# Starting every large SBUF tile at a multiple of 128 bytes in a fused attention and two-layer feed-forward kernel

## The chip, the cores and the metric

One core of one Trainium2 chip. The metric is device time in microseconds (us), the median of three runs. The engines are TensorE (PE, its weight loads listed as PEld), VectorE (DVE), ScalarE (ACT), GpSimd (POOL) and SyncE (SP), which issues nearly all DMAs.

## What is computed

Local attention with a few global keys over 4 batches, 8 heads, 768 positions and 64 head columns, and then two feed-forward layers on the 3072 x 512 result:

```python
scores = q @ k.T / 8 + bias          # bias: -slope[h] * distance
keep   = is_global | is_local        # 8 global keys, a window of 96
a      = softmax(where(keep, scores, -1e9))
x      = (a @ v) as [3072, 512]
h = x @ w1_in;  y   = (h - tanh(h)) @ w1_out     # w1_in [512, 2048]
h = y @ w2_in;  out = (h * cos(h)) @ w2_out      # w2_out [2048, 512]
```

## The kernel before

All arithmetic is float32. The feed-forward products split each operand into a high part in the type float32r and a low part (value minus high), and add three products: high x high, high x low, low x high. So each chunk of weights is a tile `w` of [128, 2, 512] (tags `wi` and `wo`, 16 buffers each), and each chunk of activations is a pair as well (`xt`, `x`, `g`).

The work goes in four phases. Phase 0 is the attention, with the first half of layer one (f chunks 0 to 7) woven into it in 12 blocks of 256 tokens: `h<-xt,wi` (L561) and `c<-g,wo` (L615), 12 matmuls of 256 columns per chunk each. A list scheduler (`Plan`, L49) with written costs and due times sets the order on each engine, and `in_order` (L32) pins it. Phases 1 to 3 are the other half of layer one and the two halves of layer two, in 6 blocks of 512 tokens and 8 chunks each: `h<-x,wi` (L561), then `o<-g,wo` (L615, phase 1) or `o<-wo,g` (L619, phases 2 and 3), 12 matmuls of 512 columns each. Per chunk the "in" matmuls go over 4 tiles of `x` and add into one accumulator `h`; the "out" matmuls take one tile `g` and add into four accumulators. Between them stand the activation (ACT, DVE) and the split of `g` (DVE, POOL). `x` is loaded from DRAM by SP ahead of use.

In the attention, `s<-kw,q` (L426) is a float32r product too: 12 matmuls on 64 partitions each, which run as six pairs, one of a pair on partitions 0 to 63 and one on 64 to 127. `tp` (L481, L385, L387) are transposes against `ident`, `x<-pt,vn` (L501) the product with v.

**Where tiles lie.** Bytes of a partition are given out from two sides, in steps of 32. From the left: 16,512 bytes of scratch and constants (129 x 128), then the pool `const` (`ident` 512, seven small tiles of 32 each, `nmall` 768; 1,504 in all), then `w`, `raw`, `p1` (phase 0: `xt`, `t`, `g`, `y`) or, later, `pb` (`t`, `g`, `s`). From the right, below byte 229,344: `pa` (in phase 0: `M`, `kw`, `kg`, `qn`, `kn`, `vn`, `q2`, `sm`, `pt`, `e`, in this order upward), later `px` (eight tiles `x`). Apart from the small ones every tile is a multiple of 128 bytes long. In the compiled program of before, the tiles begin at:

| tiles | first byte | past a multiple of 128 | past a multiple of 512 |
|---|---|---|---|
| `wo`, `wi`, `xt`, `g`, `t`, `y` (left) | 18,016 and on | 96 | 96 for `wo`, `wi`, `xt` and the `g` of phases 1 to 3 |
| `x` (right, phases 1 to 3) | 196,576 and on | 96 | 480 |
| `pt`, `e` (right) | 217,056 and on | 96 | 480 |
| `kw`, `q2` (right) | 193,408 and 212,864 | 0 | 384 |
| `M`, `qn`, `kn`, `vn`, `ident` | | 0 | |

Of the kernel before, what the change touches and what calls it, by code (L numbers as in the profile page):

```python
# [7 lines left out]
F32 = mybir.dt.float32  # L8
# [166 lines left out]
def attention_ffn_kernel(ctx, tc, q, k, v, n_global, n_local, w1_in, w1_out, w2_in, w2_out, out):  # L175
# [29 lines left out]
    const = ctx.enter_context(tc.tile_pool(name="const", bufs=1))  # L205
# [14 lines left out]
    flag = const.tile([1, 1], I32, name="flag")  # L220
    nmall = const.tile([128, NTILE * H], F32, name="nmall")

    fast = ExitStack()
    w_pool = fast.enter_context(tc.tile_pool(name="w", bufs=1))
    raw_pool = fast.enter_context(tc.tile_pool(name="raw", bufs=1))
# [3 lines left out]
    pa = sa.enter_context(tc.tile_pool(name="pa", bufs=1, side="right"))  # L229
# [127 lines left out]
    def where(i):  # L357
        return i // TB, i % TB
# [53 lines left out]
    def att_s(i, g, pool=None):  # L412

        b, t = where(i)
        a, kt = q2[i, g], kw[g]
        if pool is None:
            s = ps_a.tile([128, 2, 2, 256], F32, tag="s", name="s", bufs=1)
            s = [s[:, j] for j in range(2)]
        else:
            s = [pool.tile([128, 2, 256], F32, tag="h", name="s2", bufs=2) for j in range(2)]  # L420
        w = 128 if i == 0 else 256
        for z in range(2):
            for n, (x, y) in enumerate(((0, 0), (1, 0), (0, 1))):
                for j in range(2):
                    r = slice(64 * j, 64 * j + 64)
                    nc.tensor.matmul(s[j][:, z, 0:w], lhsT=a[r, x, z], rhs=kt[r, z, y, 0:w],  # L426
                                     start=(n == 0), stop=(n == 2))
        if t == 0:
            n, m0 = 128, 384
        else:  # L430
            n, m0 = 256, 0 if t % 2 == 0 else 128
        sm = pa.tile([128, 8], F32, tag="sm", name="sm", bufs=3)
        Sb[i, g] = (s, sm, n, m0)

    Eb = {}
# [478 lines left out]
    def plan_attention():  # L914
# [4 lines left out]
        for n, (i, g) in enumerate(quads):  # L919
# [13 lines left out]
            plan.op(("ql", i, g), "DVE", 0.9, n - 1.2, lambda i=i, g=g: qk_lo(i, g),  # L933
                    need=[("qh", i, g)], give=[(q_in, 1)])
            plan.op(("s", i, g), "PE", 0.55 if i == 0 else 0.92, n, lambda i=i, g=g, bank=bank: att_s(
                i, g, ps_h if bank == "h" else None),
                    need=[("ql", i, g)] + [("s",) + p for p in prev], take=[(bank, banks), ("sm", 1)],
# [209 lines left out]
```

## Time and profile before

| | us |
|---|---|
| median of 3 runs | 1283.38 |
| lowest, highest | 1283.26, 1283.76 |
| the profiled execution, its own time | 1282.89 |
| its span, first to last instruction | 1281.1 |

The mean granted TensorE clock of the profiled execution is 0.996. The profile is of one execution. A row of instructions gives how many there are, the time the engine was busy with them, the mean duration of one, and the idle time just before them with what ended it. Matmuls are pipelined: one starts while the one before is still draining, so the pace is read from start to start and not from the duration of one.

### The profile page before, as it was taken

What the parts mean: (1) busy time and instruction counts of PE and PEld (TensorE: products, weight loads), DVE (VectorE), ACT (ScalarE), POOL (GpSimd) and SP (SyncE); (2) the same over time, 40 slices, a digit from 0 to 9 for tenths busy, and PEclk for the clock granted to TensorE, in tenths of its full rate; (3) what the DMA queues carried; (4) which work ended last, traced back from release to release, by engine and by line L of the source; (5) the groups of instructions that cost most, each with busy time, mean ns of one, the idle gap of its engine ahead of it and who ended that gap; (6) DMA issues with size and microseconds to landing.
All of it is one profiled execution on the core that took longest, in us unless ns stands there. A gap on an engine that the chain in (4) does not pass through costs nothing.

```text
span 1281.1 us, 20646 instructions
## 1 busy us (share of the span) xinstructions
PE 1260.5 (98%) x7674; PEld 1070.4 (84%) x7677; DVE 750.2 (59%) x1709; ACT 607.5 (47%) x1407; POOL 366.3 (29%) x327
## 2 busy tenths in 40 slices
PE   8989999999999999999999999999999999999997
PEld 4789999999999998888888888888888888888886
DVE  7985666567565423434343367777775565655553
ACT  7977776667665531332333245455344333333331
POOL 0012222221221123544554342333332222222221
PEclk9999999999999999999999999999999999999999
DMA  9533344444422261654463323314220313232110
GB/s 302 154 94 97 113 121 123 121 127 112 137 57 71 63 230 52 212 169 147 144 214 128 133 101 132 115 67 148 91 91 34 132 66 110 88 129 69 66 67 36
DMA packets 160845, 149.28 MB, mean 117 GB/s; under 512 B 84960, under 2 KB 119776, under 8 KB 160736
## 3 DMA queue, kind: packets, MB, share of 16 engines
q1 hardware_dynamic: 160448, 147.88, 36.3%
q8 instruction: 62, 1.02, 0.3%
q14 instruction: 47, 0.39, 0.1%
q10 hardware_dynamic: 288, 0.00, 0.0%
HBM read 103.81 MB, written 44.04 MB: 115 GB/s over the span
## 4 chain that ended last, share of the span: by engine, by line
PE 89%; ACT 5%; DVE 4%; issue 1%; DVEq 0%; ACTq 0%
PE h L561 39%; PE o L619 20%; PE o L615 10%; PE c L615 9%; PE tp L481 3%; PE x L501 3%; PE s L426 2%; ACT e L454 2%; PE idle L825 1%; DVE e L471 1%; DVE e L446 1%; PE tp L385 1%; PE tp L387 1%; DVE wf L156 1%; DVE q L402 0%
## 5 line engine op out<-in xcount | busy, mean ns | idle before, releaser
L590 POOL TENSOR_TENSOR g<-t,g 128x512 fp32r<-128x512 f32 (+1 forms) x240 | 266.6, 1112 | 817.4 <-DVE g L585 455.1
L561 PE MATMUL h<-x,wi 128*128 128x512 f32 x1728 | 423.8, 394 | 0.0
L561 PEld LDWEIGHTS h<-x,wi 128*128 128x128 f32 x1728 | 324.0, 188 | 75.8
L619 PE MATMUL o<-wo,g 128*128 128x512 f32 x1152 | 275.5, 390 | 0.0
L619 PEld LDWEIGHTS o<-wo,g 128*128 128x128 f32 x1152 | 216.2, 188 | 47.1
L575 DVE TENSOR_TENSOR t<-h,t 128x256 f32<-128x256 f32 (+1 forms) x144 | 73.4, 511 | 179.1 <-ACT t L570 178.7
L561 PE MATMUL h<-xt,wi 128*128 128x256 f32 x1152 | 160.8, 289 | 1.0 <-ACT xt L513 0.7
L615 PE MATMUL c<-g,wo 128*128 128x256 f32 x1152 | 160.6, 286 | 0.0
L570 ACT ACTIVATE t<-h 128x256 f32<-128x256 f32 (+1 forms) x144 | 65.0, 454 | 198.0 <-PE h L561 188.7
L541 ACT ACTIVATE t<-t 128x512 f32<-128x512 f32 x96 | 60.7, 632 | 195.0 <-DVE t L540 194.8
L561 PEld LDWEIGHTS h<-xt,wi 128*128 128x128 f32 x1152 | 143.7, 190 | 4.9 <-issue 1.0
L615 PEld LDWEIGHTS c<-g,wo 128*128 128x128 f32 x1152 | 146.3, 191 | 0.3
L615 PE MATMUL o<-g,wo 128*128 128x512 f32 x576 | 139.1, 390 | 0.0
L615 PEld LDWEIGHTS o<-g,wo 128*128 128x128 f32 x576 | 108.1, 188 | 23.7
L543 DVE SCALAR_TENSOR_TENSOR t<-t,h 128x512 f32<-128x512 f32 x96 | 65.9, 686 | 100.6 <-ACT t L542 100.5
L454 ACT ACTIVATE e<-e,nmall 128x256 f32<-128x256 f32 (+1 forms) x192 | 92.4, 486 | 37.8 <-DVE nmall L446 37.8
L537 ACT ACTIVATE ki<-h 128x512 int32<-128x512 f32 x96 | 57.0, 597 | 104.6 <-PE h L561 104.2
L538 DVE SCALAR_TENSOR_TENSOR t<-ki,h 128x512 f32<-128x512 int32 x96 | 65.7, 685 | 65.6 <-ACT ki L537 65.4
L539 DVE SCALAR_TENSOR_TENSOR t<-ki,t 128x512 f32<-128x512 int32 x96 | 89.3, 930 | 2.8
L446 DVE CUSTOM_DVE_ANT_0 e<-s,M 128x256 f32<-128x256 f32 (+1 forms) x192 | 66.3, 398 | 31.7 <-PE s L426 30.9
L585 DVE CAST g<-t 128x512 fp32r<-128x512 f32 x144 | 67.8, 472 | 23.4 <-DMA yd<-g 12.0
L481 PE MATMUL tp<-ident,e 128*128 128x128 f32 x352 | 57.1, 281 | 7.7 <-ACT pt L487 3.3
(88 smaller groups left out, 1201.6 us busy)
## 6 DMA issues: line engine op xcount, KB each, us to landing
x<-yd SPq DMA_DIRECT2D x48, 512.0 KB, 5.7
raw<-in_moe_w_in_dram SPq DMA_DIRECT2D x26, 512.0 KB, 3.8
xd<-xt SPq DMA_DIRECT2D x12, 1024.0 KB, 5.4
raw<-in_moe_w_out_dram SPq DMA_DIRECT2D x24, 512.0 KB, 3.4
x<-xd SPq DMA_DIRECT2D x24, 512.0 KB, 6.6
yd<-g SPq DMA_DIRECT2D x24, 512.0 KB, 4.3
qn<-in_q_dram SPq DMA_DIRECT2D x48, 128.0 KB, 2.4
kn<-in_k_dram SPq DMA_DIRECT2D x48, 128.0 KB, 2.7
```

The lines of the kernel that those rows point to most:

```text
L446: nc.vector.tensor_tensor_reduce(out=Eb[i, g, z][:, j, 0:n], in0=s[j][:, z, 0:n], in1=M[:, z, m0:m0 + n], scale=slopes[4 * g + j] / base, ...
L454: nc.scalar.activation(out=e[:, j, 0:n], in_=e[:, j, 0:n], func=AF.Exp, scale=-1.0, bias=nmall[:, col:col + 1], accum_out=sm[:, 2 * z + j: ...
L481: nc.tensor.transpose(tp[:, 2 * c + j], e[:, j, c * 128:(c + 1) * 128], ident)
L538: mark[1] = nc.vector.scalar_tensor_tensor(out=r, in0=ki, scalar=-C1, in1=h, op0=ALU.mult, op1=ALU.add)
L539: nc.vector.scalar_tensor_tensor(out=r, in0=ki, scalar=-C2, in1=r, op0=ALU.mult, op1=ALU.add)
L543: nc.vector.scalar_tensor_tensor(out=r, in0=r, scalar=-0.5, in1=h, op0=ALU.add, op1=ALU.mult)
L561: nc.tensor.matmul(h, lhsT=wk[:, a], rhs=x[:, b], start=(kc == 0 and n == 0), stop=(kc == KC - 1 and n == 2))
L575: mark[1] = nc.vector.tensor_tensor(out=t, in0=Hb.pop((P, j, f)), in1=t, op=ALU.subtract)
L585: nc.vector.tensor_copy(out=g[:, 0], in_=Gt[P, j, f])
L590: nc.gpsimd.tensor_tensor(out=g[:, 1], in0=Gt.pop((P, j, f)), in1=g[:, 0].bitcast(F32), op=ALU.subtract)
L615: nc.tensor.matmul(o[z], lhsT=w[:, a, z * 128:(z + 1) * 128], rhs=g[:, b], start=(first and n == 0 and (P > 0 or z % 2 == 0)), stop=(last ...
L619: nc.tensor.matmul(o[z], lhsT=g[:, a, z * 128:(z + 1) * 128], rhs=w[:, b], start=(first and n == 0), stop=(last and n == 2))
```

## The change

Two tiles are allocated that nothing reads or writes, and one tag of small tiles gets a fourth buffer. No instruction of the kernel is added or removed in the source.

```diff
@@ -220,6 +220,11 @@
     nmall = const.tile([128, NTILE * H], F32, name="nmall")
+    const.tile([128, 8], F32, name="pad")
+    edge = ctx.enter_context(tc.tile_pool(name="edge", bufs=1, side="right"))
+    edge.tile([128, 24], F32, name="pad2")
...
@@ -429,7 +434,7 @@
-        sm = pa.tile([128, 8], F32, tag="sm", name="sm", bufs=3)
+        sm = pa.tile([128, 8], F32, tag="sm", name="sm", bufs=4)
```

`pad` is 32 bytes, so all left pools begin 32 bytes higher (18,048 = 141 x 128). `pad2` is 96 bytes at the right edge, so `px`, `pt` and `e` lie 96 bytes lower (`x` from 196,480 = 1,535 x 128). `sm` takes 128 bytes instead of 96, so what lies below it in `pa` (`M` to `q2`) moves down by 128 in all and stays at multiples of 128. Past a multiple of 512 the left tiles named in the table then stand at 128, `x` and `pt` at 384.

## Rows read from the trace of the kernel before

**Rows 1.** The page, busy time: engine, us (share of the span) xinstructions.
```profile
PE 1260.5 (98%) x7674; PEld 1070.4 (84%) x7677; DVE 750.2 (59%) x1709; ACT 607.5 (47%) x1407; POOL 366.3 (29%) x327
```

**Rows 2.** Busy time of each engine by stretches, with granted clock and DMA share.
```profile
core 0: us, PE busy (x) PEld busy (x) DVE busy (x) ACT busy (x) POOL busy (x), PEclk, DMA share, GB/s
0.00:50.00 50.00, 44.35 (x310) 27.86 (x313) 39.61 (x138) 41.67 (x111) 2.68 (x15) 1.00 0.96 280
50.00:100.00 50.00, 46.01 (x414) 41.66 (x415) 43.51 (x125) 41.10 (x115) 8.62 (x10) 0.97 0.29 73
150.00:200.00 50.00, 49.83 (x487) 46.43 (x484) 33.42 (x112) 34.42 (x100) 11.39 (x13) 1.00 0.42 119
500.00:600.00 100.00, 100.00 (x436) 81.51 (x435) 39.88 (x60) 28.38 (x49) 45.70 (x34) 1.00 0.43 147
800.00:900.00 100.00, 100.00 (x436) 81.49 (x436) 75.94 (x106) 48.73 (x88) 37.04 (x26) 1.00 0.30 106
```

**Rows 3.** The page, chain that ended last, shares by engine.
```profile
PE 89%; ACT 5%; DVE 4%; issue 1%; DVEq 0%; ACTq 0%
```

**Rows 4.** The page, costliest groups: the four feed-forward matmuls.
```profile
L561 PE MATMUL h<-x,wi 128*128 128x512 f32 x1728 | 423.8, 394 | 0.0
...
L619 PE MATMUL o<-wo,g 128*128 128x512 f32 x1152 | 275.5, 390 | 0.0
...
L561 PE MATMUL h<-xt,wi 128*128 128x256 f32 x1152 | 160.8, 289 | 1.0 <-ACT xt L513 0.7
...
L615 PE MATMUL c<-g,wo 128*128 128x256 f32 x1152 | 160.6, 286 | 0.0
...
L615 PE MATMUL o<-g,wo 128*128 128x512 f32 x576 | 139.1, 390 | 0.0
```

**Rows 5.** Timeline of PE in phase 1: start, us, instructions merged.
```profile
543.71 2.95 PE L561 MATMUL h<-x,wi 128*128 128x512 f32 x12
546.50 2.90 PE L615 MATMUL o<-g,wo 128*128 128x512 f32 x12
549.23 2.96 PE L561 MATMUL h<-x,wi 128*128 128x512 f32 x12
```

**Rows 6.** Timeline of PE in phase 3.
```profile
1035.61 2.90 PE L619 MATMUL o<-wo,g 128*128 128x512 f32 x12
1038.34 2.95 PE L561 MATMUL h<-x,wi 128*128 128x512 f32 x12
1041.14 2.90 PE L619 MATMUL o<-wo,g 128*128 128x512 f32 x12
```

**Rows 7.** Timeline of PE at the start: bf16 filler matmuls, then a transpose.
```profile
35.66 2.55 PE L825 MATMUL idle<-zero 128*128 128x512 bf16 x11
38.04 0.38 PE L385 MATMUL tp<-ident,qn 128*128 128x128 f32 x2
```

**Rows 8.** Timeline of PE, one `s` group: from its second pair, its last pair.
```profile
408.30 0.76 PE L426 MATMUL s<-kw,q 64*128 64x256 f32 x10
...
408.78 0.28 PE L426 MATMUL s<-kw,q 64*128 64x256 f32 x2
```

**Rows 9.** Timeline of PE, the `xt` group after: from its second, sixth, seventh matmul.
```profile
410.62 1.48 PE L561 MATMUL h<-xt,wi 128*128 128x256 f32 x11
...
411.10 0.40 PE L561 MATMUL h<-xt,wi 128*128 128x256 f32 x2
...
411.22 0.88 PE L561 MATMUL h<-xt,wi 128*128 128x256 f32 x6
```

**Rows 10.** Timeline of PE, a `c` group: two starts six matmuls apart.
```profile
411.94 1.24 PE L615 MATMUL c<-g,wo 128*128 128x256 f32 x9
...
412.66 0.88 PE L615 MATMUL c<-g,wo 128*128 128x256 f32 x6
```

**Rows 11.** Timeline of PE, an `s` group of 128 columns: third and sixth pair.
```profile
13.62 0.61 PE L426 MATMUL s<-kw,q 64*128 64x128 f32 x8
...
13.96 0.27 PE L426 MATMUL s<-kw,q 64*128 64x128 f32 x2
```

**Rows 12.** Groups of ACT and DVE by shape: results in tiles at 0 and at 96.
```profile
L396 ACT ACTIVATE kw<-tp 128x256 fp32r<-128x256 f32 x48 | 18.3, 382 | 0.0
...
L487 ACT ACTIVATE pt<-tp 128x256 f32<-128x256 f32 x16 | 6.0, 378 | 1.2 <-PE tp L481 1.2
...
L575 DVE TENSOR_TENSOR t<-h,t 128x256 f32<-128x256 f32 x96 | 40.3, 421 | 42.4 <-ACT t L570 42.0
...
L404 DVE TENSOR_TENSOR kw<-tp,kw 128x256 fp32r<-128x256 f32 x48 | 19.8, 413 | 0.0
```

**Rows 13.** The waits: those that a DMA ended.
```profile
DVE g L585 <- DMA yd<-g: 12.0, 4, 4.0
...
ACT g L634 <- DMA yd<-g: 7.6, 5, 2.8
...
ACT t L570 <- DMA ya<-y: 5.1, 1, 5.1
...
DVE nf L319 <- DMA nw<-in_n_global_dram: 4.1, 1, 4.1
...
ACT raw L139 <- DMA raw<-in_moe_w_in_dram: 1.2, 1, 1.2
```

## The prediction

> **What bounds the kernel now.** I read the page's busy times first: PE is busy for 1260.5 of 1281.1 us, and no other engine passes 59% [rows 1]. A busy PE is not a PE at its peak, so next came the busy time by stretches. In the stretches shown from 500 us on PE is busy for all of the 100 us, with 436 matmuls in them, which is 229.4 ns from one to the next; in the attention around 150 to 200 us it is busy for 49.83 of 50 us; only in the first 100 us does it lack some, 44.35 and 46.01 of 50 us, and there the DMA engines are 96% busy at first and ACT and DVE stand at 79 to 87% [rows 2]. The chain of work that ended last says the same: 89% PE, 5% ACT, 4% DVE, no DMA [rows 3]. So the kernel's time is the pace of its feed-forward matmuls: 3456 of 512 columns and 2304 of 256 [rows 4]. What an alignment of their operands is worth is therefore first a question about that pace, and a small one about ACT, DVE and DMA in the first 100 us.
>
> **The pace, and what it could hide.** In phase 1 twelve "in" matmuls start 2.79 us ahead of the "out" matmuls behind them (543.71 to 546.50), and twelve "out" 2.73 us ahead of the next "in" (546.50 to 549.23): 232.5 and 227.5 ns each [rows 5]. Phase 3 shows the same two figures, 2.73 and 2.80 us, although its "out" reads the weights as the moving operand [rows 6]. A bf16 matmul of the same 512 columns, whose operand `zero` lies at the same 96 bytes past a multiple of 128, starts every 2.38 / 11 = 216.4 ns [rows 7]. So a float32r matmul of 512 columns carries 11.1 ns ("out") or 16.1 ns ("in") more than a bf16 one. If that were the price of a start at 96 bytes, this change would take it away from 3456 matmuls; that is the large number that has to be decided.
>
> The trace has a control for it. `kw` and `q2`, the operands of `s`, are float32r tiles that lie at multiples of 128 already, while `xt`, `wi`, `g` and `wo` lie at 96. Both kinds have 256 columns. Four steps from pair to pair of `s` take 408.78 - 408.30 = 0.48 us [rows 8]; four steps of `xt` from its second matmul take 411.10 - 410.62 = 0.48 us, five take 0.60 [rows 9]; six of `c<-g,wo` take 0.72 us [rows 10]. All three are 120 ns a step. The objection is that a pair of `s` loads two sets of weights, which might hold it at 120 ns by chance. But the `s` groups of 128 columns load the same two sets per pair and go at (13.96 - 13.62) / 3 = 113 ns [rows 11], so weights do not hold the 256-column pairs at 120. With a moving operand that cost no extra, four steps would take at most 4 x 113 = 0.45 us, three times the rows' resolution of 0.01 us below the 0.48 seen. So the extra time of a float32r matmul is there with aligned operands too, and I take the gain on PE to be 0. The lower bound, if `s` is a coincidence of its half-height pairs, is the rival below.
>
> [...]
>
> **The change part by part.** `pad` and `pad2` issue nothing: no instruction, no DMA, 0 us. What they move is costed by bounds.
> - ACT and DVE. A copy of 128x256 out of PSUM takes 382 ns into aligned `kw` and 378 ns into `pt` at 96; a subtraction of the same size takes 413 ns on `kw` and 421 ns on `t` at 96 [rows 12]. The differences are 1% and 2% with opposite signs, and the operand patterns differ as well. I take 0. As bounds, 2% of DVE's 4% of the chain (51 us) is -1.0 us, and 1% of ACT's 5% (64 us) is +0.6 us [rows 3]. Elsewhere PE covers both engines: in the stretch with the most DVE work it is busy for 75.94 of 100 us [rows 2].
> - POOL has no place on the chain and is 29% busy [rows 1, 3]: 0.
> - DMA. No DMA is on the chain. The five waits that a DMA ended sum to 30.0 us [rows 13]. The first three belong to the later phases, under a PE that does not pause; `nw` lies in `const` ahead of `pad` and does not move; so only the 1.2 us of `raw` can be won. If transfers became 1% slower instead, the first 50 us, where DMA is 96% busy, are the cover that fails first: +0.5 us. I take 0, bounds -1.2 and +0.5.
> - The fourth `sm` buffer can only take away a wait for an old `sm` to be read. The 48 groups of the attention (the 48 copies into `kw`, [rows 12]) lie ahead of 500 us, so about 10 us apart: a buffer three groups old has long been read; 0. The order on each engine is pinned in phase 0, and `Plan` still counts three. Behind it PE has no gap that another order could fill.
>
> Sum: 0, with bounds of -2.2 and +1.1 us. Against the profiled execution's own time of 1282.89 us (span 1281.1 and 1.8 around it) that is 1280.7 to 1284.0; the median lies 0.5 us above that execution, so I forecast 1283.4 with 1281.2 to 1284.5 around it. About 0.2%, 2.6 us, is what a measurement of this kernel can tell from no change.
>
> **Rivals.**
> 1. *The whole float32r excess is a matter of alignment.* For it: at 512 columns the excess is 11.1 and 16.1 ns, and no 512-column operand in the trace is aligned. Against it: the control at 256 columns. Its price: 1728 x 16.1 + 1728 x 11.1 ns = 47.0 us in phases 1 to 3, and 2304 x 11.1 ns = 25.6 us in phase 0 if nothing else takes over there: 1211 to 1236 us. [...] Chance 0.05.
> 2. *Only "in" gets faster.* It is 0.06 us a group slower than "out", with the same form and widths [rows 5, 6]. What differs is that `x` lies on the right, 384 bytes from the left tiles as counted past multiples of 512 (480 against 96), and that it adds 12 times into one accumulator. In phase 0, where `xt` lies on the left, "in" also adds 12 times into one accumulator, and it goes at the same 120 ns as "out" [rows 9, 10]; that speaks for the place of `x`. The change brings the distance to 256 (384 against 128). If that ends the conflict, 144 groups x 0.06 = 8.6 us are won: 1274.8. Against it: nothing shows that distances of this kind matter, and 512 columns may be the reason. Chance 0.10.
> 3. *Only "in" gets slower.* The same dependence, the other way: the new distance doubles the excess, 2.85 us a group, +8.6 us: 1292.0. It decides from 18 ns a group on (2.6 us / 144), so from 2.81 us. "Out" cannot move by this, since all its operands are left tiles and shift together by 32 bytes. Chance 0.06.
> 4. *The first 100 us move by more than my bounds*, since nobody's cover is whole there: 3 to 5 us either way, 0.02 faster and 0.03 slower.
>
> That the change does not do what it says, if the allocator rounded otherwise, ends at the forecast too.
>
> **How the numbers follow.** The forecast has 0.74; rivals 1 and 2 and part of 4 make 0.17 faster; rival 3 and the rest of 4 make 0.09 slower. The range goes from rival 2's time, 1274, to 1286, beyond the forecast's own upper end and the spread of runs; rivals 1 and 3 and the slower part of 4, 0.14 in all, are left out.
>
> **What would show it.** In the profile after: groups of twelve at 2.79 and 2.73 us in phases 1 and 3, 436 matmuls per 100 us, 120 ns a step in phase 0, and `g`, `t`, `pt` operations of the durations of before. "In" groups at 2.73 would show rival 2, at 2.81 or more rival 3. Near 216 ns a matmul in both, some 460 per 100 us, rival 1. I would be wrong chiefly if the pairs of `s` are slow for a reason of their own.

## The result and the profile after

| | before | after |
|---|---|---|
| median, us (4 runs each) | 1283.57 | 1272.64 |
| lowest to highest | 1283.26 to 1285.14 | 1272.44 to 1273.50 |
| ratio, 95% interval | | 0.9914 [0.9897, 0.9931] |
| span of the profiled execution | 1281.1 | 1271.0 |

The change made the kernel 10.9 us faster, 0.86%. The prediction, 1283.4 us in a range of 1274 to 1286, was wrong: it had this outcome as rival 2, with a chance of 0.10 and a time of 1274.8.

In the changed kernel lines stand five further down (L566 was L561, L620 and L624 were L615 and L619). Its page, busy time and costliest groups, against [rows 1, 4]:

```profile
PE 1248.9 (98%) x7677; PEld 1069.8 (84%) x7677; DVE 750.9 (59%) x1709; ACT 606.4 (48%) x1407; POOL 365.2 (29%) x327
...
L566 PE MATMUL h<-x,wi 128*128 128x512 f32 x1728 | 413.4, 389 | 0.0
...
L624 PE MATMUL o<-wo,g 128*128 128x512 f32 x1152 | 274.9, 389 | 0.9 <-ACT y L643 0.8
...
L566 PE MATMUL h<-xt,wi 128*128 128x256 f32 x1152 | 160.9, 289 | 1.0 <-ACT xt L518 0.7
...
L620 PE MATMUL c<-g,wo 128*128 128x256 f32 x1152 | 160.5, 286 | 0.0
```

Only PE has changed, and on it almost only `h<-x,wi`: 413.4 us in place of 423.8. The 256-column matmuls stand as they did. The busy time by stretches says where:

```profile
150.00:200.00 50.00, 49.83 (x484) 46.41 (x481) 33.35 (x113) 34.56 (x100) 11.41 (x13) 1.00 0.43 120
...
500.00:600.00 100.00, 100.00 (x443) 82.81 (x442) 39.77 (x60) 28.46 (x50) 45.26 (x33) 1.00 0.43 150
...
800.00:900.00 100.00, 99.12 (x436) 81.46 (x435) 76.42 (x105) 46.94 (x85) 36.95 (x26) 1.00 0.30 102
```

The attention is as before [rows 2]. In phase 1 there are 443 matmuls per 100 us, not 436. Between 800 and 900 us there are still 436, and PE is busy for 99.12 of 100 us; before it was 100.00. The timeline of PE in phases 1 and 3, against [rows 5, 6], start and duration in us:

```profile
542.50 2.88 PE L566 MATMUL h<-x,wi 128*128 128x512 f32 x12
545.22 2.88 PE L620 MATMUL o<-g,wo 128*128 128x512 f32 x12
547.94 2.88 PE L566 MATMUL h<-x,wi 128*128 128x512 f32 x12
...
1033.77 2.88 PE L624 MATMUL o<-wo,g 128*128 128x512 f32 x12
1036.49 2.88 PE L566 MATMUL h<-x,wi 128*128 128x512 f32 x12
1039.21 2.88 PE L624 MATMUL o<-wo,g 128*128 128x512 f32 x12
```

Every group of twelve now takes 2.72 us. "In" has fallen from 2.79, "out" from 2.73: for each of 144 pairs of groups 0.08 us less by [rows 5] and 0.09 by [rows 6], so 11.5 to 13.0 us. A little of it is given back in phase 2:

```profile
868.90 5.60 PE L624 MATMUL o<-wo,g 128*128 128x512 f32 x24
874.34 5.60 PE L566 MATMUL h<-x,wi 128*128 128x512 f32 x24
880.78 3.35 PE L624 MATMUL o<-wo,g 128*128 128x512 f32 x12 [0.84 <-ACT y L643]
883.97 2.88 PE L566 MATMUL h<-x,wi 128*128 128x512 f32 x12
```

Here PE waits 0.84 us for the copy that frees its accumulators, and what is lost is more than the wait: the 60 matmuls from 868.90 to 883.97 take 15.07 us, where five groups at 2.72 take 13.60, so 1.47 us. In this stretch DVE was the busiest behind PE already, at 75.94 of 100 us [rows 2], and with a faster PE it has become the last link: the chain that ended last, 89% PE before [rows 3], now runs through DVE and ACT for the 100 us up to that point:

```profile
PE 76%; DVE 12%; ACT 6%; issue 2%; DMA 1%; SPq 1%; DVEq 0%; ACTq 0%
```

With these 1.5 us taken off, 10.0 to 11.5 us remain. From the start of the first of the 3456 matmuls of 512 columns to that of the last the trace has 814.2 us before and 803.6 after, 10.6 less; the medians differ by 10.9, the spans by 10.1.

### The profile page after: what moved, and what is told of

Same layout as the page of the kernel before. It is cut to its first block, busy times and chain, and to the rows that moved or that the text cites. A ratio compares the mean times of both kernels' runs of the same rounds, so it can differ in the third digit from the quotient of the medians.

```text
span 1271.0 us, 20649 instructions
## 1 busy us (share of the span) xinstructions
PE 1248.9 (98%) x7677; PEld 1069.8 (84%) x7677; DVE 750.9 (59%) x1709; ACT 606.4 (48%) x1407; POOL 365.2 (29%) x327
## 3 DMA queue, kind: packets, MB, share of 16 engines
q1 hardware_dynamic: 160448, 147.88, 36.6%
## 4 chain that ended last, share of the span: by engine, by line
PE 76%; DVE 12%; ACT 6%; issue 2%; DMA 1%; SPq 1%; DVEq 0%; ACTq 0%
PE h L566 32%; PE o L624 15%; PE o L620 10%; PE c L620 9%; PE tp L486 3%; PE x L506 3%; DVE t L544 2%; PE s L431 2%; ACT e L459 2%; DVE wf L156 1%; DVE t L543 1%; DVE t L548 1%; DVE t L545 1%; ACT t L547 1%; ACT t L546 1%
## 5 line engine op out<-in xcount | busy, mean ns | idle before, releaser
L566 PE MATMUL h<-x,wi 128*128 128x512 f32 x1728 | 413.4, 389 | 0.0
L566 PEld LDWEIGHTS h<-x,wi 128*128 128x128 f32 x1728 | 324.0, 188 | 67.0
L624 PE MATMUL o<-wo,g 128*128 128x512 f32 x1152 | 274.9, 389 | 0.9 <-ACT y L643 0.8
L624 PEld LDWEIGHTS o<-wo,g 128*128 128x128 f32 x1152 | 216.0, 188 | 46.8 <-ACT y L643 2.1
L566 PE MATMUL h<-xt,wi 128*128 128x256 f32 x1152 | 160.9, 289 | 1.0 <-ACT xt L518 0.7
L620 PE MATMUL c<-g,wo 128*128 128x256 f32 x1152 | 160.5, 286 | 0.0
L566 PEld LDWEIGHTS h<-xt,wi 128*128 128x128 f32 x1152 | 143.8, 191 | 4.9 <-issue 1.0
L620 PEld LDWEIGHTS c<-g,wo 128*128 128x128 f32 x1152 | 146.3, 191 | 0.3
L620 PE MATMUL o<-g,wo 128*128 128x512 f32 x576 | 138.4, 389 | 0.0
L620 PEld LDWEIGHTS o<-g,wo 128*128 128x128 f32 x576 | 108.1, 188 | 22.5
L590 DVE CAST g<-t 128x512 fp32r<-128x512 f32 x144 | 67.8, 472 | 22.8 <-DMA yd<-g 11.5
```

What stands on the lines that cost most here:

```text
L566: nc.tensor.matmul(h, lhsT=wk[:, a], rhs=x[:, b], start=(kc == 0 and n == 0), stop=(kc == KC - 1 and n == 2))
L590: nc.vector.tensor_copy(out=g[:, 0], in_=Gt[P, j, f])
L620: nc.tensor.matmul(o[z], lhsT=w[:, a, z * 128:(z + 1) * 128], rhs=g[:, b], start=(first and n == 0 and (P > 0 or z % 2 == 0)), stop=(last ...
L624: nc.tensor.matmul(o[z], lhsT=g[:, a, z * 128:(z + 1) * 128], rhs=w[:, b], start=(first and n == 0), stop=(last and n == 2))
```

## The experiments

The order of instructions on each engine is the same in the two kernels and in all experiments but the last, so only addresses differ. Three theories were set against each other: x's **own place** (or alignment), the place of the **weights** `wi`, and the **distance** between the operand that streams and the weights that are loaded meanwhile. Below, D is the first byte of `x` less that of `wi`, taken past a multiple of 256; all tiles and slices concerned repeat in steps of 512 or more, so D is one number for all "in" matmuls. "In" and "out" are start to start for twelve, in phases 1 and 3; single groups differ by 0.01 us. Totals with an interval are medians of several runs, and the ratio goes by runs of the kernel before taken beside them (medians 1283.57 to 1284.18); the others are one run each.

| kernel | x past 128 | left past 128 | D | in, us | out, us | total, us | ratio to before |
|---|---|---|---|---|---|---|---|
| before | 96 | 96 | 128 | 2.79 | 2.73 | 1283.57 | |
| after | 0 | 0 | 0 | 2.72 | 2.72 | 1272.64 | 0.9914 [0.9897, 0.9931] |
| e1_left | 96 | 0 | 96 | 2.81 | 2.76 | 1289.12 | 1.0041 [1.0027, 1.0055] |
| e2_x96 | 0 | 96 | 32 | 2.80 | 2.76 | 1287.71 | 1.0029 [1.0019, 1.0040] |
| e3_x128 | 96 | 96 | 0 | 2.72 | 2.72 | 1272.80 | 0.9908 [0.9891, 0.9924] |
| e4_sm | 96 | 96 | 128 | 2.79 | 2.73 | 1283.60 | 0.9995 [0.9986, 1.0005] |
| f1_gap | 96 | 96 | 0, but 128 for out | 2.76 in phase 1, 2.73 in phase 3 | 2.79 | 1283.82 | |
| f2_x384 | 96 | 96 | 0 | 2.72 | 2.72 | 1272.15 | |
| f3_x256 | 96 | 96 | 128 | 2.79 | 2.73 | 1282.84 | |
| f4_x64 | 32 | 96 | 64 | 2.76 | 2.77 | 1283.21 | |
| g1_after128 | 0 | 0 | 128 | 2.79 | 2.73 | 1283.23 | 0.9994 [0.9984, 1.0003] |
| g2_x192 | 32 | 96 | 192 | 2.80 | 2.74 | 1285.10 | |
| g3_x224 | 0 | 96 | 160 | 2.81 | 2.73 | 1286.94 | |
| h1_xlow | 96 | 96 | 0 high, 128 low half | 2.75 | 2.72 | 1277.57 | |

**The change taken apart.** `e1_left` makes the left half of the change alone:

```diff
     nmall = const.tile([128, NTILE * H], F32, name="nmall")
+    const.tile([128, 8], F32, name="pad")
```

> Only the 32 bytes on the left: w, g and the other left tiles begin at multiples of 128 (128 past a multiple of 512), x stays at 480 past a multiple of 512 (96 past one of 128). Theory own place (x itself must lie well for 512 columns): 'in' stays at 2.79 us a group of twelve, about 1283 us. Theory weights (the stationary operand wi must lie at a multiple of 128): 'in' falls to 2.72, about 1272.6. Theory distance (what counts is x against the left tiles; 256 apart as counted past 512 is good, 384 is bad): here it is 352, neither of the two, so it makes no call but allows any figure between 2.72 and 2.85 us.

Aligning `wi`, `g` and all other left tiles made the kernel slower, by 0.41%. The weights theory falls. The timeline of PE in phase 3 has "out" at 2.75 us in this group, 2.76 in most, and "in" at 2.81:

```profile
1028.29 2.91 PE L619 MATMUL o<-wo,g 128*128 128x512 f32 x12
1031.04 2.98 PE L561 MATMUL h<-x,wi 128*128 128x512 f32 x12
1033.85 2.92 PE L619 MATMUL o<-wo,g 128*128 128x512 f32 x12
```

`e2_x96` aligns `x` alone. The pad stands ahead of the pool of `x`, behind the attention:

```diff
+    xpad = fast.enter_context(tc.tile_pool(name="xpad", bufs=1, side="right"))
+    xpad.tile([128, 24], F32, name="pad3")
     late["px"] = fast.enter_context(tc.tile_pool(name="px", bufs=1, side="right"))
```

> Only x moves, 96 bytes down, by a pad ahead of its pool, so the attention is left as it was: x at 384 past a multiple of 512, a multiple of 128; left tiles at 96. Theory own place: 'in' falls to 2.72 us a group, about 1272.6 us in all. Theory weights: stays at 2.79, about 1283. Theory distance: 288 apart, no call.

Slower too, by 0.29%, with `x` at a multiple of 128: the own place in the sense of alignment falls. So each half of the change, taken alone, costs time; together they gain 0.86%.

`e3_x128` and the later kernels with `_x` have the same edit with 32 elements (128 bytes), or as many as their name says in bytes:

> Only x moves, 128 bytes down: it stays 96 past a multiple of 128 as all left tiles do, nothing large is aligned that was not, but its distance to the left tiles becomes 256 as counted past 512, as in the changed kernel. Theory distance: 'in' falls to 2.72 us a group, about 1272.6 us. Theory own place and theory weights: stays at 2.79, about 1283.

Only the distance theory asked for what came, 1272.80 us: the whole gain, while nothing is aligned that was not. Its timeline of PE in phase 3:

```profile
1026.83 2.88 PE L561 MATMUL h<-x,wi 128*128 128x512 f32 x12
1029.55 2.88 PE L619 MATMUL o<-wo,g 128*128 128x512 f32 x12
1032.27 2.88 PE L561 MATMUL h<-x,wi 128*128 128x512 f32 x12
```

`e4_sm` has only the third edit:

```diff
-        sm = pa.tile([128, 8], F32, tag="sm", name="sm", bufs=3)
+        sm = pa.tile([128, 8], F32, tag="sm", name="sm", bufs=4)
```

> Only the fourth sm buffer, without the two pads: the attention tiles below sm move by 32 bytes, to 96 past a multiple of 128, the rest stays. All three theories: 1283.4 us, 'in' at 2.79 and 'out' at 2.73 us a group. The s groups, whose operands are now off a multiple of 128, stay at 120 ns a step in all three; a rise of them would speak for alignment at 256 columns after all.

No difference (0.9995), as all three theories expected, although `kw` and `q2` lost their alignment here; in the trace of `e4_sm` four steps of `s` take 0.47 to 0.48 us, as before.

**All aligned, distance undone.** `g1_after128` is the reverse of `e3_x128`: the changed kernel with `x` 128 bytes lower, everything still at multiples of 128.

> The changed kernel with x alone 128 bytes lower: every large tile still begins at a multiple of 128, as the change wanted, but x and wi are 128 apart as counted past 256. Theory distance: the whole gain is gone, 'in' at 2.79 us a group, 1283.4 us. Theory alignment (starts at multiples of 128 are what pays): 2.72 and 1272.6 us.

The gain is gone to the last 0.1%: 0.9994 of the time of before. In phase 3 "in" is back at 2.79 to 2.80 us, "out" at 2.73:

```profile
1027.41 2.95 PE L566 MATMUL h<-x,wi 128*128 128x512 f32 x12
1030.21 2.90 PE L624 MATMUL o<-wo,g 128*128 128x512 f32 x12
1032.94 2.95 PE L566 MATMUL h<-x,wi 128*128 128x512 f32 x12
```

**Distance from what.** In all of these `x` or all left tiles moved. `f1_gap` moves `wi`, and `g` with it, away from `wo`:

```diff
     zero = w_pool.tile([128, 512], BF16, tag="wo", name="zero", bufs=16)
+    w_pool.tile([128, 32], F32, tag="gap", name="gap", bufs=1)
```

> A gap of 128 bytes between the wo buffers and the wi buffers: wi, and all left tiles above it (xt, g, t), move up by 128, wo and x stay; everything keeps its 96 past a multiple of 128. Theory distance (moving operand against the weights that are loaded meanwhile, counted past 256: 0 is good, 128 costs): 'in' falls to 2.72 us a group, since x and wi are now 0 apart; 'out' rises to about 2.79, since g and wo are now 128 apart; in the attention phase 'out' (c from g and wo, 256 columns), the one kind of 256-column product that is now 128 apart, rises above 120 ns a step, by an unknown amount, while xt with wi stays at 120. Total within 5 us of 1283. Theory own place (some addresses are slow for x, whatever the weights): 'in' stays at 2.79, 'out' at 2.73, 1283 us.

`x` and `wo` stay where they were, yet "in" and "out" change places: in phase 1 "in" takes 2.76 us and "out" 2.79.

```profile
543.43 2.92 PE L561 MATMUL h<-x,wi 128*128 128x512 f32 x12
546.19 2.96 PE L615 MATMUL o<-g,wo 128*128 128x512 f32 x12
548.98 2.92 PE L561 MATMUL h<-x,wi 128*128 128x512 f32 x12
```

In phase 3, where "out" streams `wo` and loads `g`, its groups take 2.79 to 2.80 as well, and "in" 2.73:

```profile
1030.27 2.96 PE L619 MATMUL o<-wo,g 128*128 128x512 f32 x12
1033.07 2.90 PE L561 MATMUL h<-x,wi 128*128 128x512 f32 x12
1035.80 2.96 PE L619 MATMUL o<-wo,g 128*128 128x512 f32 x12
1038.59 1.76 PE L561 MATMUL h<-x,wi 128*128 128x512 f32 x7
```

So the paces here go with the pair of streamed operand and weights, not with `x` and not with the accumulators. That `x` is disturbed instead by the other engines' work on `g` and `t`, which moved with `wi`, does not fit the kernel before: it has 436 matmuls per 100 us where DVE is busy for 39.88 us and where it is busy for 75.94 [rows 2].

The same run tells which weights: those that are loaded while the matmul streams, which are the next one's. In the trace of the kernel before a load starts 2 to 4 ns after the start of a 512-column matmul, bears the tiles of the matmul behind that one, and lasts 188 ns:

```profile
L561 PEld LDWEIGHTS h<-x,wi 128*128 128x128 f32 x1728 | 324.0, 188 | 75.8
```

The last "in" matmul of a group has its own weights `wi` at D = 0 in every phase of `f1_gap`. In phase 1 the load behind it is from `wo`, 128 from `x`; in phases 2 and 3 it is from `g`, which is 0 from `x`. By the starts in the trace of `f1_gap`, the step from this matmul to the next, behind nine or more "in" matmuls in a row, is 232 or 233 ns in all 38 cases of phase 1 and 226 or 227 in all 78 of phases 2 and 3. Twelve "in" take 2.76 us in the one and 2.73 in the others.

One expectation fell: in the attention phase `c<-g,wo`, 256 columns and now 128 apart, was to slow down. Busy time of its line from 100 to 500 us (the last matmuls in it are of phase 1), first `f1_gap`, then the kernel before:

```profile
100.00:500.00 400.00, 153.54 (x1080) 138.27 (x1079) 1.00 0.40 114
```

```profile
100.00:500.00 400.00, 153.87 (x1079) 138.97 (x1077) 1.00 0.39 114
```

No difference. One group of twelve and the transpose behind it, first `f1_gap`, then the kernel before, take 1.42 and 1.45 us from start to start:

```profile
402.77 1.58 PE L615 MATMUL c<-g,wo 128*128 128x256 f32 x12
404.19 0.38 PE L385 MATMUL tp<-ident,qn 128*128 128x128 f32 x2
```

```profile
402.80 1.60 PE L615 MATMUL c<-g,wo 128*128 128x256 f32 x12
404.25 0.38 PE L385 MATMUL tp<-ident,qn 128*128 128x128 f32 x2
```

So at 256 columns a distance of 128 cost nothing in `f1_gap` (153.54 against 153.87 us); other distances were not run there.

**The other distances.** 384 bytes down, D is 0 past 512 as well as past 256; 256 bytes down, it is 128 past both:

> Only x moves, 384 bytes down: 0 from the left tiles as counted past 512. Theory distance, counted past 256: as with 128 down, 'in' at 2.72 us a group, about 1272.7 us. If it must be 256 as counted past 512, 'in' is slower than that; but 'out' has been at distance 0 all along, so I expect 2.72.

> Only x moves, 256 bytes down: 128 from the left tiles as counted past 512, 128 past 256, as before. Theory distance past 256: 'in' at 2.79 us a group and 1283.4 us, as if nothing had been done. If distance counts past 512: another figure.

Both came out: 1272.15 and 1282.84 us. The timelines of phase 3, `f2_x384` and then `f3_x256`:

```profile
1025.23 2.88 PE L561 MATMUL h<-x,wi 128*128 128x512 f32 x12
1027.95 2.88 PE L619 MATMUL o<-wo,g 128*128 128x512 f32 x12
1030.67 2.88 PE L561 MATMUL h<-x,wi 128*128 128x512 f32 x12
```

```profile
1026.96 2.95 PE L561 MATMUL h<-x,wi 128*128 128x512 f32 x12
1029.75 2.90 PE L619 MATMUL o<-wo,g 128*128 128x512 f32 x12
1032.49 2.96 PE L561 MATMUL h<-x,wi 128*128 128x512 f32 x12
```

Past 512, 0 and 256 are alike (1272.15 and 1272.80 us, `f2_x384` and `e3_x128`), and so are 128 and 384 (1282.84 and 1283.57 us, `f3_x256` and the kernel before): by these four runs the period is 256 bytes. Next, 64 bytes down, and the same distances from the other side:

> Only x moves, 64 bytes down: 320 from the left tiles, 64 past 256. Theory distance: not 0, so 'in' above 2.75 us a group; the two distances off a multiple of 64 tried so far (32 and 96 past 256) gave 1287.7 and 1289.1 us, the multiple of 128 gave 1283.4; a multiple of 64 is expected between, 1283 to 1289.

> Kernel of before, only x moves, 192 bytes down: 192 past 256 from the weights. If a distance costs the same in both directions, as with 64 past 256: 1283.2 us, 'in' and 'out' both near 2.76 us a group. Alignment: x is at no multiple of 64 here; no gain.

> Kernel of before, only x moves, 224 bytes down: x begins at a multiple of 128, 160 past 256 from the weights. If a distance costs the same in both directions, as with 96 past 256: 1289 us. Theory alignment of x: 1272.6 us. No gain is expected.

At D = 64 the sum came as expected, 1283.21, with "out" slowed as much as "in" sped up. The symmetry did not: D = 192 gave 1285.10 in place of 1283.2, with 2.80 and 2.74 us, and D = 160 gave 1286.94 in place of 1289. The only good place found is 0; the other six that were run (32 to 192; 224 was not) lie between 1282.8 and 1289.1 us. "Out", whose own distance is 0 in all of these, takes 2.73 to 2.77 us at the other six places, and 2.72 where "in" is at 0.

**One matmul at a time.** In `h1_xlow` the high half of `x` is at D = 0 and the low half at 128. Of every three "in" matmuls the second reads the low half.

```diff
-        t = late["px"].tile([128, 2, N2], F32R, tag="x", name="x", bufs=8)
+        t = late["px"].tile([128, 2, N2 + 32], F32R, tag="x", name="x", bufs=7)[:, :, 0:N2]
```

(with a pad of 128 bytes ahead of the pool)

> x tiles get 128 unused bytes behind each half (seven buffers in place of eight, for room): the high half of x is 0 from wi past 256, the low half 128. Of three 'in' matmuls one reads the low half. Theory distance, if it is the matmul that streams against the weights loaded meanwhile: only the steps of those that read the low half lengthen, so 'in' gets about a third of the excess of 0.07 us a group: 2.74 to 2.75 us. If what counts were the first tile start alone: 2.72; if the excess came from 'in' as a whole: 2.79. The total depends on whether seven buffers hold up the loads of x: 1275 to 1285 us.

"In" takes 2.75 us and "out" 2.72, as the distance theory asked:

```profile
1032.50 2.88 PE L619 MATMUL o<-wo,g 128*128 128x512 f32 x12
1035.22 2.91 PE L561 MATMUL h<-x,wi 128*128 128x512 f32 x12
1037.97 2.88 PE L619 MATMUL o<-wo,g 128*128 128x512 f32 x12
```

That makes (2.75 - 2.72) / 4, about 8 ns, for each of four steps, and the starts in the trace show which: of every three steps (227, 234 and 226 ns, medians) only that of the matmul that streams the low half is long. The total, 1277.57, lies higher than the 4.3 us that this adds to the best kernel: PE pauses a little, 0.7 us of it for a load of `x` with one buffer less, and the order of instructions differs here.

## Why the prediction was wrong

**The step that failed** is the control: "So the extra time of a float32r matmul is there with aligned operands too, and I take the gain on PE to be 0." Its first half holds: with everything aligned a step of 512 columns still takes 226.7 ns (2.72 us for twelve in the changed kernel), against 216.4 for bf16 [rows 7]. Its second half does not follow from it, because the control compared two cases that were both undisturbed. The pairs at 256 columns are `kw` with `q2`, `xt` with `wi`, and `g` with `wo`: 193,408 less 212,864, 161,376 less 83,552 and 180,832 less 18,016 are all multiples of 256. All three are at D = 0, so nothing in the control was at the distance of 128 that "in" had. And a pair at 128 would not have been slower there, as `f1_gap` showed at 256 columns. The control was a good one for alignment and blind for what the change did. So the term of the sum that was wrong is that of PE: put at 0, it was 10.6 us, the time that the matmuls of 512 columns gained.

**What the runs showed in its place.** A start at a multiple of 128 was worth nothing: `e3_x128` has the gain without it (0.9908), `g1_after128` has it without the gain (0.9994). The pads changed D for `x` and `wi` from 128 to 0, as a by-product of two shifts of 32 and 96 bytes. That is rival 2 in place and sign. It was given 0.10 because nothing but one difference of 5 ns between "in" and "out" [rows 5, 6] spoke for it; that difference, between two forms of equal work, was the strongest sign in the trace and weighed too little.

**Rival 2's size** was 8.6 us, from "in" falling to the 2.73 of "out". "In" fell to 2.72, and "out" with it; 0.08 to 0.09 us for each of 144 pairs is 11.5 to 13.0. "Out" was itself held back by the "in" groups beside it, so it was no clean floor: by the starts in the trace of the kernel before, its first three steps behind an "in" group take 232, 232 and 231 ns and the other nine 227; after the change all twelve take 226 or 227. For the same reason rival 3's sentence that "out" cannot move was wrong: with `x` alone moved it took up to 2.77 us.

**Rival 3** (a worse distance) did not happen with the change, but exists: 1287.7 and 1289.1 us in `e2_x96` and `e1_left`. **Rival 1** is false: the paces fell to 226.7 ns, not to 216, and stay there with everything aligned.

**The terms taken as 0** held. ACT, DVE and POOL have the busy time of before (606.4, 750.9 and 365.2 us after 607.5, 750.2 and 366.3 [rows 1]), the attention too (PE 49.83 us busy from 150 to 200 us in both), DMA stands the same (the queue with nearly all of its bytes took 36.3% of the 16 engines' span before and 36.6% after), and the fourth `sm` buffer alone gave 0.9995 [0.9986, 1.0005]. What I had not foreseen is the 1.5 us given back where DVE takes over from PE in phase 2: "Elsewhere PE covers both engines" held for the pace of before and not quite for the faster one.

**What stays open.** Why 256 bytes, why the slowing was seen at 512 columns and not at 256, and why it lasts for three more steps in the group behind. The traces show that weights are loaded while a matmul streams (a load starts 2 to 4 ns after it) and that the step goes with the distance between the two (2.72 us for twelve at D = 0, 2.76 to 2.81 at the other six places); by what means, they do not show. Whether a matmul's own weights count besides the next one's was not separated. The distances with one run each rest on that run and its timeline. A version better than both kernels was not found: moving `x` alone by 128 bytes (`e3_x128`, 0.9908) does as well as the whole change.

## What to carry to other kernels

When two groups of matmuls of the same form and width go at different paces, compare the addresses of their two operands: in this kernel a distance of 0 past 256 bytes, instead of 128, between the moving tile and the weights loaded meanwhile was worth 0.9% (`e3_x128`, 0.9908), and one unused tile of 128 bytes bought it. Before a control is trusted, ask whether it differs from the case in the thing that the change touches; here alignment differed and the distance did not. And test a pad from each side alone, since two shifts that each cost time can gain together.

## What was not expected of the hardware

- In this kernel the pace of float32r matmuls of 512 columns went with the distance in SBUF between the moving operand and the weights that are loaded meanwhile, those of the next matmul: twelve "in" took 2.72 us at 0 past 256 bytes (the changed kernel, `e3_x128`, `f2_x384`) and 2.76 to 2.81 at 32, 64, 96, 128, 160 and 192 (`e2_x96`, `f4_x64`, `e1_left`, the kernel before, `g3_x224`, `g2_x192`). At 256 columns a distance of 128 cost nothing: 1080 matmuls of `c<-g,wo` were busy for 153.54 us in `f1_gap`, 1079 for 153.87 in the kernel before.
- The slowing reached the group beside: "out" at its own distance of 0 took 2.73 (the kernel before) to 2.77 us (`f4_x64`) next to "in" groups at the other distances, and 2.72 next to those at 0 (the changed kernel). With "in" at 128 the excess lay in the first three steps of "out": 232, 232 and 231 ns against 227 for the other nine, in the kernel before.
- Twelve took 2.72 us at best (the changed kernel, `e3_x128`, `f2_x384`), 226.7 ns each; with 256 columns it was 120.0 ns [rows 10]. An estimate from these two steps: the 256 columns between them take 106.7 ns, which is 2.4 columns a ns at a granted clock of 1.00 [rows 2] and leaves 13.3 ns of each step beyond its columns. No run here had a lower pace at 512 columns, at any distance or alignment.
